# Attention's products with the values: from split parts in float32r to plain float32, two heads side by side in TensorE's column halves

## The chip, the cores and the metric

The kernel runs on one NeuronCore of a Trainium2 chip. The metric is the time of one execution on the device in microseconds (us), the median of several runs.

## The reference, cut to what matters

Three layers follow each other. The first is attention over 4 batches, 8 heads, 576 positions and 64 numbers per head, with rotary positions; it is the only layer that the change rewrites.

```python
q_rot, k_rot = (rotate(q), rotate(k))
scores = scale * np.matmul(q_rot, k_rot.transpose(0, 1, 3, 2))
scores = scores - np.max(scores, axis=-1, keepdims=True)
attn = np.exp(scores)
attn = attn / (np.sum(attn, axis=-1, keepdims=True) + 1e-09)
return np.matmul(attn, v).astype(np.float32)
```

Its output, with the heads put side by side, is the input of a gated feed-forward layer (`_moe_ref`), and that one's output is the input of a causal attention with four experts (`_moe2_ref`).

## The kernel before

The kernel has three stages, one for each layer. TensorE's fast format float32r rounds its operands, so each operand is split in a high part (rounded) and a low part (what rounding took away), and a product is made from two or three products of parts.

**Stage A, attention.** A *work* is a pair of heads of one batch: 16 works, numbered n = 0 to 15. A work has nine *slots* x = 0 to 8, one for each block of 128 query rows (blocks 0 to 3 of both heads in turn; slot 8 holds the last 64 rows of both). `slot(k)` writes the instructions of one slot, and they keep that order on each engine. In slot x of a work the kernel does these things, the stages of neighbouring blocks overlapping:

- `exps(x)`: ScalarE (ACT) reads the score bank `ps_S` and the negative row maximum `nmax` and writes the exponentials `e`.
- `turn(x-1)`: TensorE (PE) transposes the block before, four 128x128 pieces, `ps_t<-ident,e`.
- `scores(x+1)`: PE makes the next block's scores into one of the **two** `ps_S` banks (four products of 288 columns; six for x+1 = 8).
- `maxima(x+1)`: VectorE (DVE) takes the maximum of each row of that bank.
- `turn_left` (`ps_l`): five times a work PE transposes the last 64 columns of two blocks, which DVE has gathered (`gather`).
- `high`, `low`: ACT copies the transposed block, rounded, out of PSUM (`g00h`, `g01h` for the first 256 query rows of either head, `g1h` for the other 320 of both); DVE subtracts that from PSUM to get the low part (`g00l`, `g01l`, `g1l`). `left_high` and `left_low` do so for the left-over columns (`tlh`, `tll`).
- `av`: the products with the values, into `ps_o`, a single bank. `vst` holds the values' high part in its first 64 columns and the low part in the last 64, so one product of 128 columns gives both. A head's first 256 (or last 320) rows take ten products: five blocks of keys times two parts of the exponentials. They are written in two pieces, four products in one slot and six in the next: first half of the rows in slots 6, 7 and 8, 0; second half, for the work before, in slots 2, 3 and 4, 5.
- `av_out`: ACT copies `ps_o` to `xt`, and `store` writes it to memory (`xr`), high and low rows apart; they are added later.

`values` (ACT and GpSimd, POOL) makes `vst` from the loaded values `v`. Beside this, POOL rotates the queries and keys of the work after the next, DVE and POOL split them (`hi`, `lo`), DMAs on SyncE's queue (SP) spread the parts to the places where TensorE needs them, and in works with odd n the first layer's weights are unpacked (`wt`, four DVE operations and two of ACT for each of eight pieces, loaded into the single buffer `raw`).

**Stage B** starts with `attended`, which reads `xr` back, adds its two parts (`sa<-sa,sl`, on POOL), multiplies by the softmax factors (`sa<-sa,sr`) and splits the result (`xh`, `xl`). For batch 0 that already happens in stage A. **Stage C** is the third layer; no line of it is touched.

On each engine instructions run in the order in which they stand: a waiting one holds up all behind it.

Of the kernel before, what the change touches and what calls it, by code (L numbers as in the profile page):

```python
# [8 lines left out]
F32 = mybir.dt.float32  # L9
# [8 lines left out]
P = 128  # L18
HS = 288
NP = H // 2  # L20
NKB = 5
# [5 lines left out]
def f(ap):  # L27

    return ap.bitcast(F32)
# [11 lines left out]
def fused_kernel(ctx, tc, qk, v, w_in, w_out, w_sg, g_ln, b_sg, wqk, wvg, wo, rope, cst, out):  # L41
# [37 lines left out]
    xraw = [spill.tile([2, 4, P, S], F32, name=f"xr{b}") for b in range(B)]  # L79
# [200 lines left out]
    def attended(pool, b):  # L280


        ts = {}

        def load(c):
            ts[c] = a, l, r = [pool.tile([P, S], F32, tag="s" + x, name="s" + x, bufs=k)
                               for x, k in (("a", 3), ("l", 1), ("r", 1))]
            for x, t in enumerate((a, l)):
                nc.sync.dma_start(t, xraw[b][x, c])
            factor_in(r, rd[b][c])  # L290
            POOL.tensor_tensor(a, a, l, op=ALU.add)

        def norm(c):
            a, l, r = ts[c]
# [14 lines left out]

    def leftover(pool, b):  # L310

        a, l, r = [pool.tile([P, S], F32, tag="s" + x, name="e" + x, bufs=k)[:, 0:512]
                   .rearrange("p (c i n) -> p c i n", c=4, i=2) for x, k in (("a", 3), ("l", 1), ("r", 1))]
        for i in range(2):
            for x, t in enumerate((a, l)):
                nc.sync.dma_start(t[:, :, i, :], xraw[b + i][x, :, :, 512:S].rearrange("c p n -> p c n"))
# [4 lines left out]
        POOL.tensor_tensor(a, a, l, op=ALU.add)  # L321
# [13 lines left out]
    with ExitStack() as st:  # L335
# [12 lines left out]
        prs = [Pair(opd, x, zero, True) for x in range(2)]  # L348


        g0 = [[ptp.tile([P, 4, 256], F32R, name=f"g0{j}{x}") for x in "hl"] for j in range(2)]
        g1 = [ptp.tile([P, 4, 640], F32R, name="g1" + x) for x in "hl"]


        tl = [ptp.tile([P, 640], F32R, name="tl" + x) for x in "hl"]

        def ends(t):

# [6 lines left out]
        class Work:  # L365
# [17 lines left out]
                    nc.sync.dma_start(ident, cst[:, 0:P])  # L383

            def load_values(self):
                self.vt = ld.tile([P, NKB, 2, D], F32, tag="v", name="v", bufs=1)
                nc.sync.dma_start(self.vt, v[self.b, self.p])

            def first(self):
# [26 lines left out]
                else:  # L416
                    self.pr.fill_k(opd, hi, lo)

            def values(self):
                self.vst = ld2.tile([P, NKB, 2, P], F32R, tag="vst", name="vst")  # L420
                ACT.copy(self.vst[:, :, :, 0:D], self.vt)
                POOL.tensor_tensor(self.vst[:, :, :, D:P], self.vt, f(self.vst[:, :, :, 0:D]), op=ALU.subtract)

            def start(self):
                self.nmax, self.sums = [sm.tile([P, 9], F32, tag=x, name=x) for x in ("nmax", "sums")]
                self.ps, self.e, self.t4 = {}, {}, {}
# [24 lines left out]
                    PE.transpose(t4[:, kb, :], self.e[x][:, P * kb:P * kb + P], ident)  # L451

            def place(self, x):
                i, j = divmod(x, 2)
                hi, lo = g0[j] if i < 2 else g1
                off = P * i if i < 2 else P * (i - 2) + (320 if j else 64)
                if i < 4:
                    return self.t4[x], *[x[:, :, off:off + P] for x in (hi, lo)]
                return self.t4[x].rearrange("p k (j n) -> p k j n", j=2), *[ends(x) for x in (hi, lo)]
# [19 lines left out]
            def left_parts(self, second):  # L479
                c = slice(256, 640) if second else slice(0, 256)  # L480
                return self.l[:, 0:c.stop - c.start], *[x[:, c] for x in tl]

            def left_high(self, second):
                i, hi, lo = self.left_parts(second)
                ACT.copy(hi, i)

            def left_low(self, second):
                i, hi, lo = self.left_parts(second)
                DVE.tensor_tensor(lo, i, f(hi), op=ALU.subtract)

            def av(self, second, j, part):

                n = 320 if second else 256
                if part == 0:
                    self.o = bank("o")
                mms = [(self.vst[:, kb, j, :], g1[x][:, kb, 320 * j:320 * j + n] if second else g0[j][x][:, kb])
                       for x in range(2) for kb in range(4)]
                mms += [(self.vst[:, 4, j, :], t[:, 256 + 64 * j:S + 64 * j] if second else t[:, 0:256]) for t in tl]
                for x, (w, m) in enumerate(mms):
                    if (x >= 4) == part:  # L500
                        PE.matmul(self.o[:, 0:n], w, m, start=(x == 0), stop=(x == len(mms) - 1))

            def av_out(self, second, j):
                n = 320 if second else 256
                if j == 0:
                    self.xt = wk.tile([P, 2, n], F32, tag=f"xt{n}", name="xt", bufs=1)
                todo = [(0, 0, n)]
                if second and j == 0:
                    todo = [(256, 0, 64), (0, 64, 256)]
                for c, i, m in todo:  # L510
                    ACT.copy(self.xt[:, j, c:c + m], self.o[:, i:i + m])

            def factor(self, step):
                if step == 0:
# [8 lines left out]
            def store_factor(self):  # L523
                factor_out(wk, self.l[0:9, 384:512], rd[self.b][self.p])

            def store(self, second):
                c = slice(256, S) if second else slice(0, 256)
                for x in range(2):
                    nc.sync.dma_start(xraw[self.b][x, self.p].rearrange("(j p) s -> p j s", j=2)[:, :, c],
                                      self.xt[64 * x:64 * x + 64])  # L530

        def slot(k):


# [32 lines left out]
            if n == 0 and x == 3:  # L567
                works[1].rope(1, (2,), DVE)
            if wk:
                wk.high(xk)  # L570
                wk.low(xk)
            if x == 0 and p:
                p.factor(1)
            if x == 2 and p:
                p.left_high(True)
                p.store_factor()
                p.left_low(True)
            if x == 5 and w:
                w.left_high(False)
                w.left_low(False)  # L580
# [24 lines left out]

# [17 lines left out]
        works[1].load(1)  # L623
        fixed[0] = True
        works[1].rope(0)
        works[0].values()
        works[1].load_values()
        works[1].rope(1, (0, 1))
        works[0].start()
        works[0].scores(0)  # L630
# [806 lines left out]
```

## Time and profile before

| | |
|---|---|
| median of 3 runs | 738.38 us (736.77 to 738.62) |
| the profiled execution | 739.81 us, of which the profile's span is 738.0 us |
| busy shares over the span | PE 92%, weight loads (PEld) 86%, DVE 77%, ACT 64%, POOL 53% |
| DMA | 121.51 MB, 165 GB/s in the mean |
| stage A | about 0 to 300 us |

A profile is one execution as the hardware profiler saw it. Times in it count from the span's start. Matmuls are pipelined, and their recorded durations overlap; what a matmul costs TensorE is the distance to the next one's start. The chain of waits follows back from the last instruction to what released it, step by step. The clock is the one that the throttle granted to TensorE (1.00 is full).

### The profile page before, as it was taken

Reading aid. Unit: us, or ns where it says so; the run is one execution under the profiler, and the core shown is the slowest. Engines: PE = TensorE matmul, PEld = TensorE weight load, DVE = VectorE, ACT = ScalarE, POOL = GpSimd, SP = SyncE. Lnnn points to the kernel's source line nnn. Section 1 sums busy time; section 2 is a strip of 40 time slices with the busy share of each in tenths; the row PEclk is TensorE's granted clock in tenths of the full one; section 3 lists DMA queues with packets and bytes.
Section 4 is the critical chain, followed back from the end, with each engine's and each line's share of the span. In section 5 each row is a group of like instructions: output and inputs, shape, how many; then the busy total and the mean of one; then the engine's idle time right before and its main releaser. Section 6 shows DMA issues by size and latency. Waiting matters only on the chain.

```text
span 738.0 us, 14204 instructions
## 1 busy us (share of the span) xinstructions
PE 679.6 (92%) x4813; PEld 636.6 (86%) x4813; DVE 566.1 (77%) x1234; ACT 471.0 (64%) x1183; POOL 391.5 (53%) x311
## 2 busy tenths in 40 slices
PE   6899998987899999989779999998998989999987
PEld 6788898987798988888669999898998979999975
DVE  5799999996999999588996676556337786766774
ACT  7688898986798988543343442564226756666662
POOL 2798888986889962455624835603503340432220
PEclk9899999999999999999999999999999999999999
DMA  6689878879688963534546444304465354443521
GB/s 241 191 232 275 261 218 268 230 237 272 177 240 250 246 180 111 146 127 139 184 143 203 129 134 143 90 1 149 104 196 136 93 144 117 108 119 75 138 74 65
DMA packets 70410, 121.51 MB, mean 165 GB/s; under 512 B 19489, under 2 KB 28546, under 8 KB 70338
## 3 DMA queue, kind: packets, MB, share of 16 engines
q1 hardware_dynamic: 67602, 114.93, 53.6%
q10 hardware_dynamic: 2736, 5.68, 2.5%
q8 instruction: 39, 0.64, 0.4%
q14 instruction: 33, 0.27, 0.1%
HBM read 63.20 MB, written 23.70 MB: 118 GB/s over the span
## 4 chain that ended last, share of the span: by engine, by line
PE 55%; DVE 26%; ACT 6%; DMA 5%; POOL 3%; issue 3%; SPq 1%; DVEq 0%; ACTq 0%; POOLq 0%
PE ps_S L55 31%; PE ps_t L55 9%; PE ps_o L55 9%; DVE nmax L55 5%; DVE wt L55 4%; PE ps_f L55 4%; POOL t L55 2%; PE ps_s L55 2%; DVE g1l L55 2%; DVE hi L55 2%; ACT e L55 2%; ACT qz L55 2%; DVE g01l L55 1%; DVE g00l L55 1%; DVE e L55 1%
## 5 line engine op out<-in xcount | busy, mean ns | idle before, releaser
L55 PE MATMUL ps_t<-ident,e 128*128 128x128 f32 x776 | 127.2, 281 | 21.9 <-ACT e L55 17.6
L55 ACT ACTIVATE e<-ps_S,nmax 128x576 f32<-128x576 f32 x144 | 108.2, 751 | 31.6 <-DVE nmax L55 30.5
L55 PEld LDWEIGHTS ps_t<-ident,e 128*128 128x128 f32 x776 | 92.1, 143 | 35.8 <-ACT e L55 26.5
L55 DVE TENSOR_REDUCE nmax<-ps_S 128x1 f32<-128x576 f32 x144 | 107.5, 746 | 13.6 <-PE ps_S L55 11.5
L55 POOL TENSOR_TENSOR t<-t,rp 128x576 f32<-128x576 f32 x61 | 91.5, 1521 | 14.3 <-ACT rp L55 9.2
L55 PE MATMUL ps_S<-kh,q 128*128 128x288 f32 x352 | 85.1, 335 | 2.5 <-ACT kh L55 2.4
L55 PE MATMUL ps_S<-lo,qz 128*128 128x288 f32 x304 | 66.6, 301 | 1.5 <-DVE lo L55 1.5
L55 POOL TENSOR_TENSOR lo<-t,hi 128x576 fp32r<-128x576 f32 x30 | 43.0, 1433 | 33.0 <-DVE hi L55 33.0
L55 DVE TENSOR_TENSOR g1l<-ps_t,g1h 128x512 fp32r<-128x512 f32 x80 | 54.6, 683 | 2.2 <-ACT g1h L55 2.0
L55 PEld LDWEIGHTS ps_S<-kh,q 128*128 128x128 f32 x352 | 53.4, 195 | 2.8 <-ACT kh L55 2.5
L55 ACT ACTIVATE e<-e,nmax 128x128 f32<-128x128 f32 (+4 forms) x72 | 42.3, 587 | 21.0 <-DVE nmax L55 20.7
L55 POOL TENSOR_TENSOR yl<-x,yh 128x640 fp32r<-128x640 f32 x16 | 25.0, 1568 | 55.5 <-ACT yh L55 35.8
L55 PEld LDWEIGHTS ps_S<-lo,qz 128*128 128x128 f32 x304 | 49.9, 193 | 1.7 <-DVE lo L55 1.7
L55 POOL TENSOR_TENSOR xl<-sa,xh 128x576 fp32r<-128x576 f32 x16 | 27.2, 1711 | 38.5 <-ACT xh L55 38.5
L55 ACT CAST g1h<-ps_t 128x512 fp32r<-128x512 f32 x80 | 47.2, 590 | 0.0
L55 ACT ACTIVATE ga<-ga 128x512 f32<-128x512 f32 (+1 forms) x34 | 22.3, 657 | 33.4 <-DVE ga L55 33.2
L55 POOL TENSOR_TENSOR t<-t 128x576 f32<-128x576 f32 x29 | 41.8, 1441 | 2.3
L55 DVE CUSTOM_DVE_ANT_0 e<-ps_s,mask 128x128 f32<-128x128 f32 (+3 forms) x64 | 31.0, 486 | 8.7 <-PE ps_s L55 8.3
L55 POOL TENSOR_TENSOR xt<-xt,r 128x256 f32<-128x256 f32 (+1 forms) x14 | 11.3, 805 | 48.9 <-DMA r<-d 48.9
L55 PE MATMUL ps_S<-wsh,vh 128*128 128x288 f32 x160 | 34.9, 300 | 2.3 <-DVE u L55 1.8
L55 PE MATMUL ps_S<-xh,wih 128*128 128x288 f32 x128 | 29.1, 311 | 7.0 <-DVE gv L55 4.4
L55 PE MATMUL ps_S<-wsl,vh 128*128 128x288 f32 x160 | 34.1, 294 | 0.0
(296 smaller groups left out, 2204.9 us busy)
## 6 DMA issues: line engine op xcount, KB each, us to landing
t<-in_qk_dram SPq DMA_DIRECT2D x32, 576.0 KB
kh<-hi SPq DMA_DIRECT2D x92, 144.0 KB
q<-hi SPq DMA_DIRECT2D x38, 144.0 KB
qz<-hi SPq DMA_DIRECT2D x38, 144.0 KB
q<-lo SPq DMA_DIRECT2D x38, 144.0 KB
v<-in_v_dram SPq DMA_DIRECT2D x16, 320.0 KB
xr<-xt SPq DMA_DIRECT2D x32, 160.0 KB
sa<-xr SPq DMA_DIRECT2D x16, 288.0 KB
```

The lines of the kernel that those rows point to most:

```text
L55: ins = op(*a, **k)
```

## The change

Exponentials and values are no longer split. A transposed block is copied once, as plain float32, by ACT or, for x = 1, 4 and 7, by DVE. The values are used as loaded, `v` with two buffers in place of one, and loaded in slot 5. The products with the values are plain float32 with 64 columns of weights: head 0 writes partitions 0 to 63 of `ps_o`, head 1 partitions 64 to 127, in turn, so that both heads of a pair stand side by side in the array's column halves. All ten products of one half of the rows stand in one slot: slot 3 for the second half of the work before, slot 6 for the first half. `av_out` and `store` follow at the start of slots 4 and 7. `xr` holds one part, and the addition on POOL is gone in `attended` and `leftover`.

```diff
         def load(c):
-            ts[c] = a, l, r = [pool.tile([P, S], F32, tag="s" + x, name="s" + x, bufs=k)
-                               for x, k in (("a", 3), ("l", 1), ("r", 1))]
-            for x, t in enumerate((a, l)):
-                nc.sync.dma_start(t, xraw[b][x, c])
+            ts[c] = a, r = [pool.tile([P, S], F32, tag="s" + x, name="s" + x, bufs=k) for x, k in (("a", 3), ("r", 1))]
+            nc.sync.dma_start(a, xraw[b][c])
             factor_in(r, rd[b][c])
-            POOL.tensor_tensor(a, a, l, op=ALU.add)
...
             def load_values(self):
-                self.vt = ld.tile([P, NKB, 2, D], F32, tag="v", name="v", bufs=1)
+                self.vt = ld.tile([P, NKB, 2, D], F32, tag="v", name="v")
...
-            def values(self):
-                self.vst = ld2.tile([P, NKB, 2, P], F32R, tag="vst", name="vst")
-                ACT.copy(self.vst[:, :, :, 0:D], self.vt)
-                POOL.tensor_tensor(self.vst[:, :, :, D:P], self.vt, f(self.vst[:, :, :, 0:D]), op=ALU.subtract)
...
             def place(self, x):
+
                 i, j = divmod(x, 2)
-                hi, lo = g0[j] if i < 2 else g1
+                o, t = g0[j] if i < 2 else g1, self.t4[x]
...
-            def high(self, x):
-                i, hi, lo = self.place(x)
-                ACT.copy(hi, i)
-
-            def low(self, x):
-                i, hi, lo = self.place(x)
-                DVE.tensor_tensor(lo, i, f(hi), op=ALU.subtract)
+                (DVE.tensor_copy if x % 3 == 1 else ACT.copy)(o, t)
...
-            def av(self, second, j, part):
+            def av(self, second):
 
                 n = 320 if second else 256
-                if part == 0:
-                    self.o = bank("o")
...
+                self.o = bank("o")
+                for kb in range(NKB):
+                    for j in range(2):
+                        if kb == 4:
+                            m = tl[:, 256 + 64 * j:S + 64 * j] if second else tl[:, 0:256]
+                        else:
+                            m = g1[:, kb, 320 * j:320 * j + n] if second else g0[j][:, kb]
+                        PE.matmul(self.o[64 * j:64 * j + 64, 0:n], self.vt[:, kb, j, :], m, start=(kb == 0), stop=(kb == 4))
...
-            for at, g, second, j in ((1, p, False, 1), (4, p, True, 0), (6, p, True, 1), (8, w, False, 0)):
+            for at, g, second in ((4, p, True), (7, w, False)):
                 if x == at and g:
-                    g.av_out(second, j)
-            if x in (1, 6) and p:
-                p.store(x == 6)
+                    g.av_out(second)
+                    g.store(second)
...
-            for at, g, second, j in ((2, p, True, 0), (4, p, True, 1), (6, w, False, 0), (8, w, False, 1), (-1, p, False, 1)):
-                if x in (at, at + 1) and g:
-                    g.av(second, j, x - at)
+            for at, g, second in ((3, p, True), (6, w, False)):
+                if x == at and g:
+                    g.av(second)
...
-                if x == 6:
-                    nx.values()
-                    if n + 2 < B * NP:
-                        works[n + 2].load_values()
+                if x == 5:
+                    nx.load_values()
```

What this does to the order is seen best on TensorE. These are its rows of the kernel before from slot 3 to slot 6 of a work (`ps_t` transposes, `ps_S` scores, `ps_l` left-overs, `ps_o` products with the values):

```order
L55 MATMUL ps_o<-g1h,vst 128x320 x4
L55 MATMUL ps_t<-ident,e 128x128 x4
L55 MATMUL ps_S<-kh,q_1_172 128x288 x2
L55 MATMUL ps_S<-lo_410,qz_173 128x288 x2
L55 MATMUL ps_l<-ident,e 128x128
L55 MATMUL ps_o<-g1l,vst 128x320 x4
L55 MATMUL ps_o<-tlh,vst 128x320
L55 MATMUL ps_o<-tll,vst 128x320
L55 MATMUL ps_t<-ident,e 128x128 x4
L55 MATMUL ps_S<-kh,q_1_172 128x288 x2
L55 MATMUL ps_S<-lo_410,qz_173 128x288 x2
L55 MATMUL ps_o<-g00h,vst 128x256 x4
```

Four or six products with the values stand between any two blocks. In the changed kernel the same place of a work, from slot 3 to slot 6 (`g_196` is `g1`, `g_194` is the first of `g0`), reads:

```order
L55 MATMUL ps_o<-g_196,v 64x320 x8
L55 MATMUL ps_o<-tl,v 64x320 x2
L55 MATMUL ps_t<-ident,e 128x128 x4
L55 MATMUL ps_S<-kh,q_1_172 128x288 x2
L55 MATMUL ps_S<-lo_808,qz_173 128x288 x2
L55 MATMUL ps_l<-ident,e 128x128
L55 MATMUL ps_t<-ident,e 128x128 x4
L55 MATMUL ps_S<-kh,q_1_172 128x288 x2
L55 MATMUL ps_S<-lo_808,qz_173 128x288 x2
L55 MATMUL ps_l<-ident,e 128x128
L55 MATMUL ps_t<-ident,e 128x128 x4
```

All ten products of both heads now stand in one piece, and between the next blocks nothing stands but one left-over.

On SP's queue the load of the values stood behind the loads of queries and keys and ahead of a load of weights (`raw`). Before, at the change from work 8 to 9:

```order
L529 DMA xr_64<-xt 64x2x320 x2
L374 DMA t_2714<-in_qk_dram 128x1152
L374 DMA t_2716<-in_qk_dram 128x1152
L387 DMA v<-in_v_dram 128x640
L227 DMA raw<-in_w_in_dram 128x1024
L529 DMA xr_65<-xt 64x2x256 x2
```

In the changed kernel, at the same place:

```order
L492 DMA xr_64<-xt 64x320
L382 DMA v<-in_v_dram 128x640
L369 DMA t_2354<-in_qk_dram 128x1152
L369 DMA t_2356<-in_qk_dram 128x1152
L492 DMA xr_65<-xt 128x256
L227 DMA raw<-in_w_in_dram 128x1024
```

The values moved ahead, and `raw` now stands behind the store of the first half's output.

## Rows read from the trace of the kernel before

**Rows 1.** Busy us by stretch: PE, PEld, DVE, ACT, POOL; clock, DMA share, GB/s.
```profile
100.00:120.00 20.00, 19.19 (x150) 18.22 (x149) 19.09 (x37) 18.05 (x47) 18.81 (x14) 1.00 0.87 246
...
440.00:460.00 20.00, 20.00 (x152) 20.00 (x151) 13.33 (x19) 6.79 (x11) 9.44 (x7) 1.00 0.37 125
```

**Rows 2.** Chain of waits in 87 to 121 us: start, length, what.
```profile
95.36 0.11 PE ps_l L55
95.47 0.59 PE ps_o L55 x4
96.05 0.44 PE ps_t L55 x4
96.49 0.53 PE ps_S L55 x4
...
97.13 0.88 PE ps_o L55 x6
...
99.92 0.80 PE ps_S L55 x6
...
102.51 0.48 PE ps_o L55 x4
...
104.06 0.71 PE ps_o L55 x6
```

**Rows 3.** ACT's timeline, the one `rs` of each work, in its slot 0.
```profile
87.88 0.20 ACT L55 ACTIVATE rs<-sums 128x9 f32<-128x9 f32 x1
...
104.07 0.20 ACT L55 ACTIVATE rs<-sums 128x9 f32<-128x9 f32 x1
...
121.21 0.20 ACT L55 ACTIVATE rs<-sums 128x9 f32<-128x9 f32 x1
...
171.81 0.20 ACT L55 ACTIVATE rs<-sums 128x9 f32<-128x9 f32 x1
...
196.43 0.20 ACT L55 ACTIVATE rs<-sums 128x9 f32<-128x9 f32 x1
```

**Rows 4.** The tile `rs`: durations (min/median/max ns), first and last start.
```profile
L55 ACT ACTIVATE rs<-sums x16: 198/201/228, 37.2 to 295.7; 128x9 f32<-128x9 f32 x16
```

**Rows 5.** TensorE's warm-up by forms, plain float32, 5.4 to 6.6 and 1 to 9 us.
```profile
L55 PE MATMUL ps_l<-zero 128*128 128x128 f32 x13 | 1.6, 275 | 0.0
...
L55 PE MATMUL ps_l<-zero 128*64 128x128 f32 x32 | 2.0, 276 | 0.0
L55 PEld LDWEIGHTS ps_l<-zero 128*64 128x64 f32 x32 | 1.7, 137 | 0.1
```

**Rows 6.** Groups of 0 to 330 us: busy us, mean ns of one.
```profile
L55 DVE TENSOR_TENSOR g1l<-ps_t,g1h 128x512 fp32r<-128x512 f32 x80 | 54.6, 683 | 2.2 <-ACT g1h L55 2.0
...
L55 DVE SCALAR_TENSOR_TENSOR wt<-raw,wt 128x512 int32<-128x512 int32 x16 | 20.1, 1254 | 0.0
```

**Rows 7.** The tile `ob`: a plain float32 copy by DVE.
```profile
L55 DVE COPY ob<-ps_f x1: 693/693/693, 723.0 to 723.0; 128x512 f32<-128x512 f32 x1
```

**Rows 8.** Timeline, 101 to 104 and 152 to 153.5 us: from scores to transposes.
```profile
101.73 0.51 PE L55 MATMUL ps_S<-kh,q 128*128 128x288 f32 x2
...
102.55 0.76 DVE L55 TENSOR_REDUCE nmax<-ps_S 128x1 f32<-128x576 f32 x1 [0.30 <-PE ps_S L55]
...
103.34 0.74 ACT L55 ACTIVATE e<-ps_S,nmax 128x576 f32<-128x576 f32 x1 [0.18 <-DVE nmax L55]
...
152.44 0.74 ACT L55 ACTIVATE e<-ps_S,nmax 128x576 f32<-128x576 f32 x1 [0.95 <-DVE nmax L55]
...
153.32 0.31 PEld L55 LDWEIGHTS ps_t<-ident,e 128*128 128x128 f32 x3 [1.01 <-ACT e L55]
```

**Rows 9.** Chain of waits in work 9, 165 to 185 us.
```profile
171.21 6.96 DMA raw<-in_w_in_dram
```

**Rows 10.** Timeline of stage B, POOL and PE.
```profile
348.11 1.89 POOL L55 TENSOR_TENSOR sa<-sa,sl 128x576 f32<-128x576 f32 x1
...
355.64 0.50 PE L55 MATMUL ps_t<-wih,xl 128*128 128x512 f32 x1 [2.27 <-POOL xl L55]
```

More of the change, by code (lines that the diff above doesn't have):

```diff
@@ L77, in fused_kernel @@
     ident = cpool.tile([P, P], F32, name="ident")
-    xraw = [spill.tile([2, 4, P, S], F32, name=f"xr{b}") for b in range(B)]
+    xraw = [spill.tile([4, P, S], F32, name=f"xr{b}") for b in range(B)]
     rd = [spill.tile([4, 9, P], F32, name=f"rd{b}") for b in range(B)]
@@ L310, in leftover @@
     def leftover(pool, b):
-        a, l, r = [pool.tile([P, S], F32, tag="s" + x, name="e" + x, bufs=k)[:, 0:512]
-                   .rearrange("p (c i n) -> p c i n", c=4, i=2) for x, k in (("a", 3), ("l", 1), ("r", 1))]
+        a, r = [pool.tile([P, S], F32, tag="s" + x, name="e" + x, bufs=k)[:, 0:512]
+                .rearrange("p (c i n) -> p c i n", c=4, i=2) for x, k in (("a", 3), ("r", 1))]
         for i in range(2):
-            for x, t in enumerate((a, l)):
-                nc.sync.dma_start(t[:, :, i, :], xraw[b + i][x, :, :, 512:S].rearrange("c p n -> p c n"))
+            nc.sync.dma_start(a[:, :, i, :], xraw[b + i][:, :, 512:S].rearrange("c p n -> p c n"))
             for j in range(2):
@@ L320, in leftover @@
                 nc.sync.dma_start(r[h, :, i, :], d.to_broadcast([64, 4, 64]))
-        POOL.tensor_tensor(a, a, l, op=ALU.add)
         yield
@@ L348, in fused_kernel @@
         prs = [Pair(opd, x, zero, True) for x in range(2)]
-        g0 = [[ptp.tile([P, 4, 256], F32R, name=f"g0{j}{x}") for x in "hl"] for j in range(2)]
-        g1 = [ptp.tile([P, 4, 640], F32R, name="g1" + x) for x in "hl"]
-        tl = [ptp.tile([P, 640], F32R, name="tl" + x) for x in "hl"]
+        g0 = [ptp.tile([P, 4, 256], F32, name=f"g0{j}") for j in range(2)]
+        g1 = ptp.tile([P, 4, 640], F32, name="g1")
+        tl = ptp.tile([P, 640], F32, name="tl")
         def ends(t):
@@ L454, in place @@
                 i, j = divmod(x, 2)
-                hi, lo = g0[j] if i < 2 else g1
+                o, t = g0[j] if i < 2 else g1, self.t4[x]
                 off = P * i if i < 2 else P * (i - 2) + (320 if j else 64)
                 if i < 4:
-                    return self.t4[x], *[x[:, :, off:off + P] for x in (hi, lo)]
-                return self.t4[x].rearrange("p k (j n) -> p k j n", j=2), *[ends(x) for x in (hi, lo)]
-            def high(self, x):
-                i, hi, lo = self.place(x)
-                ACT.copy(hi, i)
-            def low(self, x):
-                i, hi, lo = self.place(x)
-                DVE.tensor_tensor(lo, i, f(hi), op=ALU.subtract)
+                    o = o[:, :, off:off + P]
+                else:
+                    o, t = ends(o), t.rearrange("p k (j n) -> p k j n", j=2)
+                (DVE.tensor_copy if x % 3 == 1 else ACT.copy)(o, t)
             def gather(self, i):
@@ L477, in turn_left, with place_left @@
                 PE.transpose(o, self.e[2 * i][:, 512:640], ident)
-            def left_parts(self, second):
+            def place_left(self, second):
                 c = slice(256, 640) if second else slice(0, 256)
[L481 to L489, printed above, removed]
@@ L491, in av @@
-            def av(self, second, j, part):
-                n = 320 if second else 256
-                if part == 0:
-                    self.o = bank("o")
[L496 to L501, printed above, removed]
@@ L503, in av_out @@
-            def av_out(self, second, j):
-                n = 320 if second else 256
[L505 to L511, printed above, removed]
+                ACT.copy(tl[:, c], self.l[:, 0:c.stop - c.start])
@@ new lines, in av @@
+            def av(self, second):
+                n = 320 if second else 256
+                self.o = bank("o")
[3 more added lines that the diff above has]
+                            m = tl[:, 256 + 64 * j:S + 64 * j] if second else tl[:, 0:256]
+                        else:
+                            m = g1[:, kb, 320 * j:320 * j + n] if second else g0[j][:, kb]
+                        PE.matmul(self.o[64 * j:64 * j + 64, 0:n], self.vt[:, kb, j, :], m, start=(kb == 0), stop=(kb == 4))
@@ new lines, in av_out, with store @@
+            def av_out(self, second):
+                n = 320 if second else 256
+                self.xt = wk.tile([P, n], F32, tag=f"xt{n}", name="xt", bufs=1)
+                ACT.copy(self.xt, self.o[:, 0:n])
+            def store(self, second):
+                o, t = xraw[self.b][self.p], self.xt
+                if second:
+                    todo = [(o[0:64, 256:512], t[0:64, 64:320]), (o[0:64, 512:S], t[0:64, 0:64]), (o[64:P, 256:S], t[64:P, :])]
+                else:
+                    todo = [(o[:, 0:256], t)]
+                for a, c in todo:
+                    nc.sync.dma_start(a, c)
@@ L524, in store_factor @@
                 factor_out(wk, self.l[0:9, 384:512], rd[self.b][self.p])
[L526 to L530, printed above, removed]
         def slot(k):
@@ L569, in slot @@
             if wk:
-                wk.high(xk)
-                wk.low(xk)
+                wk.place(xk)
             if x == 0 and p:
@@ L574, in slot @@
             if x == 2 and p:
[L575 removed]
+                p.place_left(True)
                 p.store_factor()
[L577 removed]
             if x == 5 and w:
[L579 to L584 removed]
+                w.place_left(False)
+            for at, g, second in ((3, p, True), (6, w, False)):
+                if x == at and g:
+                    g.av(second)
             if nx:
@@ L625, in fused_kernel @@
         works[1].rope(0)
-        works[0].values()
-        works[1].load_values()
         works[1].rope(1, (0, 1))
```

2 lines of the change are left out of this document (1 added, 1 removed).

## The prediction

> **What bounds the kernel now.** I read the busy time by stretch first. In stage A all engines are full [rows 1]: of 20 us TensorE is busy 19.2, VectorE 19.1, ScalarE 18.1 and POOL 18.8; in stage B TensorE is busy throughout and the others wait for it. So the change must pay in stage A, and busy shares don't say on which engine. The chain of waits does. In works with even n, where no weights are unpacked, it runs on TensorE alone, block after block [rows 2]: 0.44 us of transposes, 0.53 of scores (0.80 where six products make them), 0.11 for a left-over, and a piece of the products with the values, 0.59 and 0.88 us for the second half of the rows, 0.48 and 0.71 for the first. One work has 9 x 0.44 + 8 x 0.53 + 0.80 + 6 x 0.11 (five left-overs and the factors) = 9.66 us without the values, and 2 x (0.59 + 0.88 + 0.48 + 0.71) = 5.32 with them: 14.98 us of TensorE. A work takes 16.2 us where n is even (87.88 to 104.07) and 17.1 where it is odd [rows 3]; the extra is VectorE's, which unpacks weights in between. Over works 1 to 15 it is 258.5 us [rows 4], one of them, work 9, with 24.6 [rows 3]. So TensorE is 1.2 us (n even) and 2.1 us (n odd) of a work from its own floor, and relief of the other engines can bring no more than that, unless TensorE's work itself shrinks.
>
> **TensorE's work after the change.** Twenty products in plain float32 with 64 columns of weights take the place of forty in float32r. The trace has this form, in the warm-up. A plain float32 matmul is issued as two pieces. With the full array 13 of 128 columns take 1.6 us [rows 5], (1.6 - 0.275) / 12 = 0.11 us a piece. In column halves 32 pieces take 2.0 us: as the last one's 0.276 is mostly its own length, 16 steps in some 1.75 us, 0.11 us for two pieces. So the halves do run side by side, and two heads cost what one would. With the columns in proportion (the fixed part of a step counted along, so this is the upper end; without any, 4% less) a pair of pieces takes 0.22 us at 256 columns and 0.275 at 320. Ten pairs each: 2.2 and 2.75 us. Going into the halves and out of them, four times a work, has no row of its own: between nothing and one weight load that lies open, 0.137 us [rows 5]; I take 0.09, nearer the upper end, since the array has to run empty: 0.36. Sum 9.66 + 4.95 + 0.36 = 14.97 us. TensorE's work stays what it was.
>
> By the Trainium skill's page TensorE: Matmul & The Clock Gate (Part 3, on packing small matmuls) a weight load overlaps running matmuls only where their row groups differ, which halves of the columns do not offer; by it every step would also pay a weight load, and the sum would be the 790 us of the third rival. Here 32 loads of 0.137 us, 4.4 us in all, lie within the 2.0 us of their matmuls [rows 5], so the trace speaks against it.
>
> **What the others are relieved of.** VectorE loses nine subtractions of 0.68 us [rows 6] and two smaller ones, and gains three copies; the nearest row for such a copy, out of PSUM at the end of the kernel, says 0.69 [rows 7]. That is 4 to 5 us of a work. ScalarE loses a third of its copies, the rounding of the values and half of `av_out`, and POOL the values' low part. None of this counts by itself: as the sum above shows, TensorE would still need 14.97 us. It matters by what TensorE waits for.
>
> **What is late next.** The two score banks allow a lead of one block. From the start of a block's scores 0.82 us pass to the maxima (101.73 to 102.55), 0.79 to the exponentials, 0.88 to the block's first transposes (152.44 to 153.32) [rows 8]: 2.49 us, in which TensorE must find other work. In order it has that block's own scores (0.53), the transposes of the block before (0.44) and the scores of the block after (0.53), 1.50 us, and what else stands in these two slots. So for each two neighbouring blocks TensorE waits 0.99 us, less what else stands there. Before the change there is a piece of the products with the values in eight slots of nine, 0.48 to 0.88 us, and so almost every such sum is covered. After it, slots 3 and 6 have everything, and the others a left-over of 0.11, or (slot 1) two. The sums of neighbouring waits, by the slot in which the later block's scores stand: slots 4 and 5, 0.99 - 0.22 = 0.77; 7 and 8, 0.88 (the six products of slot 7 lengthen both sides); 8 and 0, 0.88; 0 and 1, 0.66; 1 and 2, 0.77; none across slots 3 and 6. The least that satisfies all is 0.77 + 0.88 + 0.77 = 2.42 us. Followed in order, with ScalarE's `xt` copy standing ahead of the exponentials of slots 4 and 7 so that they wait for the burst, I get 2.5. A work then takes 14.97 + 2.5 = 17.5 us, against 16.2.
>
> In the eight odd works an operation of the unpacking stands on VectorE between the maxima of slot 8's block and the next. Before, it lengthened VectorE's row; now VectorE is idle in the bursts, and only this place counts: of its 1.25 us [rows 6] 0.83 would reach TensorE, 0.27 if it runs undisturbed by POOL; I take 0.55. That makes 18.05 against 17.1.
>
> **What comes back.** Work 9 lost 7.5 us: ScalarE waited for weights whose load was issued behind the values' load, which waited for POOL, and took 6.96 us to land [rows 9]. Now the values wait for nobody, but the load stands behind the store of slot 7, which waits for the burst. It is issued about 0.9 us after the second burst (the copy `xt`, the store) and lands 7 us later; ScalarE comes to it in slot 1, by the working above some 6 us after the burst. I leave 1.9 us of the loss. In stage B POOL's addition of 1.89 us stands ahead of the `xl` for which TensorE waited 2.27 us [rows 10]; without it TensorE starts 1.9 earlier, and as it is full later on [rows 1], that stays. The other additions lie beside a busy TensorE and give nothing. The store's third DMA and the values' load now stand ahead of the loads of queries and keys; I cost them at nothing, since their rotation is used only in slots 1 and 3 of the next work, some 8 us later; were that cover gone, it is the second rival below.
>
> **The sum.** Works 1 to 15: 7 x 17.5 + 8 x 18.05 + 1.9 = 268.8, against 258.5: +10.3. Less 1.9 in stage B: +8.4. The profiled execution, 739.8 (span 738.0 and 1.8 around it), becomes 748.2; the median of the runs lies 1.4 lower, so 746.8. I say 746.5.
>
> **The rivals.**
> *TensorE is kept fed* (the other side). What must fall is the 2.5 us a work. For it: these waits are sums of latencies, and a shorter queue on VectorE and ScalarE shortens them; TensorE may also load weights of the next scores during a wait. Against it: the three latencies are already those of places where no queue stood before. If half of them goes, 15 x 1.25 = 19 us come off: 728. If all goes, 709. It decides from waits under 2.5 - 8.4 / 15 = 1.9 us a work.
> *The queue slips.* Loads of queries and keys come behind three stores that wait for the burst; if the rotation on POOL is late for slots 1 and 3, 1 us a work more: 762.
> *The halves don't overlap so well with real operands.* In the warm-up both halves read one tile; here each has its own. With weight loads in the open, 20 steps x 0.137 = 2.7 us a work, 790. With the halves one after the other, 4.95 us a work, 826. Against it stand the warm-up's rows.
>
> **How the numbers follow.** A measurement of this kernel tells about 0.3% from no change, 2.2 us. Forecast (waits as worked out, 738 to 757): 0.54, of which 0.46 slower, 0.06 the same and 0.02 faster. TensorE fed, 709 to 738: 0.26, of which 0.03 the same. The queue: 0.12. Halves: 0.08. So slower 0.66, same 0.09, faster 0.25. The forecast's own range, 738 to 757, follows from 0.3 us a work either way for the latencies and 0.27 to 0.83 for the unpacking. For 8 in 10 the range reaches to half of the waits, with a little beyond for a faster work 9, and to the queue's case: 726 to 763; outside lie the halves' 0.08 and the ends of the two others.
>
> **What would show it.** Right: steps of 0.22 and 0.275 us in the products with the values; busy VectorE and ScalarE in stage A well below 15 of 20 us; transposes waiting for exponentials some 2.5 us a work, mainly in slots 5, 6, 8, 1 and 2 and none after slots 3 and 6; works of 17 to 18 us; work 9 no longer apart. Wrong: works under 16.5 us with TensorE without gaps, or bursts of 5 us and more.

## The result and the profile after

| | before | after |
|---|---|---|
| median | 738.36 us (736.77 to 738.62, 4 runs) | 746.65 us (745.91 to 751.36, 4 runs) |
| ratio after to before | | 1.013, 95% interval 1.0086 to 1.0175 |
| span of the profiled execution | 738.0 us | 744.5 us |
| first and last of the 16 `rs` | 37.2 and 295.7 us | 35.3 and 312.4 us |
| from the last `rs` to the end | 442.3 us | 432.1 us |

The kernel became slower by 1.3%, 8.3 us, where 746.5 us were predicted. The two last lines show that this is a difference of two larger numbers: works 1 to 15 take 18.6 us more (277.1 against 258.5), and what follows takes 10.2 less; 1.9 more came back ahead of work 0's `rs`, where the granted clock of the kernel before was 0.50 from 28.9 to 32.3 us and the changed kernel's 1.00 (no run separates the two). The prediction had +10.3 and -1.9 in the two main places, so its sum stands on two errors of opposite sign.

Busy time by stretch (PE, PEld, VectorE, ScalarE, POOL), answering [rows 1]:

```profile
100.00:120.00 20.00, 17.72 (x131) 13.20 (x130) 12.55 (x25) 13.22 (x35) 12.81 (x10) 1.00 0.68 188
440.00:460.00 20.00, 20.00 (x152) 20.00 (x151) 15.29 (x35) 8.68 (x15) 4.67 (x3) 1.00 0.35 110
```

In stage A no engine is full any more. VectorE falls from 19.1 to 12.6 of 20 us, ScalarE from 18.1 to 13.2, and TensorE, which nothing relieved, from 19.2 to 17.7: it waits. The period of a work, from ScalarE's timeline and the tile's summary (durations in ns, first and last start), answering [rows 3, 4]:

```profile
71.84 0.20 ACT L55 ACTIVATE rs<-sums 128x9 f32<-128x9 f32 x1
90.71 0.20 ACT L55 ACTIVATE rs<-sums 128x9 f32<-128x9 f32 x1
108.20 0.20 ACT L55 ACTIVATE rs<-sums 128x9 f32<-128x9 f32 x1
127.06 0.20 ACT L55 ACTIVATE rs<-sums 128x9 f32<-128x9 f32 x1
145.48 0.20 ACT L55 ACTIVATE rs<-sums 128x9 f32<-128x9 f32 x1
```
```profile
L55 ACT ACTIVATE rs<-sums x16: 198/201/218, 35.3 to 312.4; 128x9 f32<-128x9 f32 x16
```

A work with odd n takes 18.87 us (71.84 to 90.71), one with even n 17.49 (90.71 to 108.20). Works 6, 8 and 10 take 18.4 to 18.7 (127.06 to 145.48). The chain of waits through half a work, answering [rows 2]:

```profile
75.66 0.66 PE ps_t L55 x4
76.31 0.53 PE ps_S L55 x4
76.84 2.84 PE ps_o L55 x20
79.69 0.59 PE ps_t L55 x4
80.27 0.55 PE ps_S L55 x4
...
80.85 0.77 DVE nmax L55
...
81.70 0.84 ACT e L55 x2
...
82.58 0.66 PE ps_t L55 x4
83.24 0.53 PE ps_S L55 x4
83.77 2.31 PE ps_o L55 x20
```

Before, the chain ran on TensorE alone. Now it leaves TensorE once between the two bursts: scores at 80.27, maxima, exponentials, and the block's transposes at 82.58. The bursts themselves take 2.84 and 2.31 us, and the transposes behind them 0.59 where they took 0.44 [rows 2]. What TensorE waits for from 30 to 300 us, by the table of waits (us in total, times, longest):

```profile
PE ps_t L55 <- ACT e L55: 28.5, 59, 1.4
```

### The profile page after: what moved, and what is told of

Same layout as the page of the kernel before. It is cut to its first block, busy times and chain, and to the rows that moved or that the text cites. A ratio compares the mean times of both kernels' runs of the same rounds, so it can differ in the third digit from the quotient of the medians.

```text
span 744.5 us, 13802 instructions
## 1 busy us (share of the span) xinstructions
PE 681.0 (91%) x4813; PEld 587.1 (79%) x4813; DVE 486.6 (65%) x1106; ACT 428.3 (58%) x1071; POOL 336.6 (45%) x277
## 4 chain that ended last, share of the span: by engine, by line
PE 65%; DVE 17%; ACT 10%; issue 3%; DMA 3%; POOL 1%; SPq 1%; ACTq 0%; DVEq 0%; POOLq 0%
PE ps_S L55 32%; PE ps_o L55 15%; PE ps_t L55 12%; ACT e L55 5%; DVE nmax L55 5%; PE ps_f L55 4%; DVE wt L55 3%; PE ps_s L55 2%; DMA raw<-in_w_in_dram 2%; ACT qz L55 2%; DVE e L55 1%; ACT wt L55 1%; DVE ga L55 1%; DMA qz<-hi 1%; DVE sa L55 1%
## 5 line engine op out<-in xcount | busy, mean ns | idle before, releaser
L55 PE MATMUL ps_t<-ident,e 128*128 128x128 f32 x776 | 129.6, 284 | 38.9 <-ACT e L55 36.8
L55 PEld LDWEIGHTS ps_t<-ident,e 128*128 128x128 f32 x776 | 86.8, 141 | 79.0 <-ACT e L55 61.2
L55 POOL TENSOR_TENSOR t<-t,rp 128x576 f32<-128x576 f32 x61 | 88.0, 1464 | 14.2 <-ACT rp L55 9.2
L55 PE MATMUL ps_o<-g,v 128*64 128x320 f32 (+1 forms) x512 | 69.2, 412 | 0.0
L55 ACT COPY g<-ps_t 128x512 f32<-128x512 f32 x96 | 55.5, 579 | 0.2 <-PE ps_t L55 0.2
L55 PEld LDWEIGHTS ps_o<-g,v 128*64 128x64 f32 x512 | 34.0, 137 | 24.4 <-issue 5.3
L55 ACT COPY xt<-ps_o 128x256 f32<-128x256 f32 (+1 forms) x32 | 12.8, 399 | 63.3 <-PE ps_o L55 63.3
```

The lines of the kernel that those rows point to most:

```text
L55: ins = op(*a, **k)
```

## The experiments

Each is the changed kernel with an edit, except the one marked as the kernel before. Those of one run only (2, 7, 9 and 10) are read by their traces. Ratios are to the kernel before, run beside them. "Works" are distances between `rs`; "even" is a work with even n and nothing of batch 0's multiplication in it.

**1. The bursts dealt out over eight slots.**

```diff
+        PARTS = ((0,), (1,), (2,), (3, 4))
-                for kb in range(NKB):
+                for kb in PARTS[part]:
-            for at, g, second in ((4, p, True), (7, w, False)):
+            for at, g, second in ((5, p, True), (0, p, False)):
-            for at, g, second in ((3, p, True), (6, w, False)):
-                if x == at and g:
-                    g.av(second)
+            for at, g, second in ((1, p, True), (5, w, False)):
+                if 0 <= x - at < 4 and g:
+                    g.av(second, x - at)
```

> The changed kernel, with each burst of products dealt out over four slots: keys' blocks 0, 1, 2 and 3 with 4 in slots 1 to 4 (second half of the rows) and 5 to 8 (first half). Theory (TensorE waits because most slots have no filler): the waits for exponentials, 2.7 us in a work with even n, nearly all go; TensorE's own work rises by the six further times that it goes into the column halves and out of them, 0.05 + 0.09 us each, to 9.66 + 4.91 + 1.12 = 15.7 us. Works of 15.7 to 16.1 us (even) and at most 17 (odd), in place of 17.5 and 18.9; 746.7 less 7 x 1.6 less 8 x 1.9 = 720 us, between 712 and 728. First rival (the waits come from queues on VectorE and ScalarE, not from missing filler): works stay at 17.3 or more, 743 to 750. Second rival (going into and out of the halves costs far more once it happens eight times a work): works of 18 us and more, over 750.

Measured: 729.76 us, ratio 0.987 (0.9839 to 0.9902). A stretch of the chain of waits:

```profile
90.10 0.59 PE ps_t L55 x4
90.68 0.53 PE ps_S L55 x4
91.21 0.69 PE ps_o L55 x4
91.90 0.58 PE ps_t L55 x4
...
103.30 0.64 PE ps_t L55 x4
```

The chain is on TensorE alone again, and works with odd and with even n take the same 17.08 us: the waits are gone but for 0.2 us (below), and with them the price of the unpacking. So the first rival (queues on VectorE and ScalarE) falls. The expected 15.7 us a work was too low, because each trip into the column halves costs more than the 0.14 us that I had read at the two ends of a burst. A slot now takes 0.59 + 0.53 + 0.69 = 1.81 us, with 0.15 of the trip in the transposes behind it. Two kernels give both unknowns. In the changed one products and two trips cost 2.84 + 2.31 + 2 x 0.15 = 5.45 us. In this one 17.08 - 9.66 = 7.42 us hold the products, eight trips and 0.20 us of slot 0, where no piece stands and the transposes take 0.64 in place of 0.44 (the last row). A trip is (7.42 - 0.20 - 5.45) / 6 = 0.30 us, the products alone 4.9. Works 6, 8 and 10 took 17.96: VectorE's multiplication for batch 0 stands between two blocks' maxima at the end of slot 8, where slot 0 has no products.

**2. One head after the other.**

```diff
-                for kb in range(NKB):
-                    for j in range(2):
+                for j in range(2):
+                    for kb in range(NKB):
```

> The changed kernel, with all five products of head 0 ahead of the five of head 1 in a burst; nothing else. Theory (the two column halves run at the same time, and only neighbouring pieces of different halves overlap): the pieces of one head follow each other at 0.269 and 0.222 us, so the bursts take up to 20 x 0.269 = 5.4 and 20 x 0.222 = 4.4 us in place of 2.84 and 2.31; at 4.7 us more in each of 15.5 works about 815 us, 790 to 825. Rival (a piece of 64 columns takes half the time of a full one wherever it stands): bursts as before, 746 us.

Measured: 792.56 us. TensorE's timeline of one burst:

```profile
83.37 2.42 PE L55 MATMUL ps_o<-g,v 128*64 128x320 f32 x10
85.57 0.43 PE L55 MATMUL ps_o<-tl,v 128*64 128x320 f32 x1
85.63 0.43 PE L55 MATMUL ps_o<-g,v 128*64 128x320 f32 x1
85.84 0.43 PE L55 MATMUL ps_o<-tl,v 128*64 128x320 f32 x1
85.90 1.51 PE L55 MATMUL ps_o<-g,v 128*64 128x320 f32 x5
87.25 0.70 PE L55 MATMUL ps_o<-tl,v 128*64 128x320 f32 x2
87.88 0.66 PE L55 MATMUL ps_t<-ident,e 128*128 128x128 f32 x4
```

Head 0 has eight pieces `g` and two `tl`. Its eight take 85.57 - 83.37 = 2.20 us, 0.275 each, and five of head 1 take 87.25 - 85.90 = 1.35, 0.27 each: one piece alone costs what a pair costs when the heads take turns (below). So the halves do work at the same time, and only pieces of different halves that stand close to each other overlap; the rival falls. The time is below the expected 815 because TensorE doesn't keep strictly to the order in which the products are written: ten `g` have begun by 85.57, two of them of head 1, and the two `tl` of head 0 stand between further `g` of head 1. Some four steps overlap at the seam. The burst is 4.51 us long in place of 2.85, the other one 3.66 in place of 2.31 (91.95 to 95.61); together 3.0 more, and works with even n go from 17.48 to 20.49.

**3. The unpacking and batch 0's multiplication behind the bursts.**

```diff
-            if x in ((1, 3, 4, 6, 7, 8) if n % 2 else (7,)):
-                next(wload, None)
+            for at in ((3, 3, 3, 6, 6) if n % 2 else (3, 3) if n else (7,)):
+                if x == at:
+                    next(wload, None)
-            if n >= 4 and x == 8:
+            if n >= 5 and x == 6:
```

> The changed kernel, with the unpacking of the weights and the steps of batch 0's multiplication moved to the end of slots 3 and 6, behind the bursts, where VectorE and ScalarE stand idle for 1.5 to 2.9 us. Theory (these operations cost time only because they stand between two blocks' maxima or ahead of exponentials, 1.4 us in odd works and 0.9 at the starts of works 6, 8 and 10): all works go to 17.4 to 17.8 us, 8 x 1.3 + 3 x 0.9 = 13 us less, 734 us (731 to 738). Rival (they cost time through the engine's load or its shared port, wherever they stand): no change, 743 to 750.

Measured: 741.88 us, ratio 1.0044 (1.0016 to 1.0071): 4.8 us less than the changed kernel, not 13. Works 6, 8 and 10 fell to 17.7, as the other even ones, though the multiplication takes 1.36 us here: beside a burst it costs nothing (experiment 7 shows what it meets at its old place). Odd works fell to 18.33 only, and the other even ones, which now hold two steps of the unpacking in place of one, rose from 17.48 to 17.69. VectorE's timeline in slot 3:

```profile
77.22 3.17 DVE L55 TENSOR_SCALAR wt<-wt 128x512 f32<-128x512 f32 x2 [0.22 <-ACT wt L55]
80.31 1.43 DVE L55 TENSOR_REDUCE nmax<-ps_S 128x1 f32<-128x576 f32 x2
```

Two operations, 0.42 and 1.25 us long in the changed kernel, take 3.17 here, while POOL is busy throughout, and outlast the burst; the maxima of the next block come behind them.

**4. POOL's additions put back.**

```diff
             factor_in(r, rd[b][c])
+            POOL.tensor_tensor(pool.tile([P, S], F32, tag="sl", name="sl", bufs=1), a, a, op=ALU.subtract)
```

(and the same in `leftover`).

> The changed kernel with an operation on POOL put back where the additions stood (a subtraction of the same shape from itself into the tile that held the low part, its result unused, no further load). It prices the additions alone. Theory (the additions held up VectorE and POOL at the start of stage B beyond the one place that was costed): stage A unchanged (277 us from work 0 to work 15), the way from there to the first steady products of stage B longer by 6 to 9 us, 753 to 756 us. Rival (only the one addition ahead of the late low part counts; the rest of what stage B regained comes from elsewhere, such as weights unpacked further ahead): 748 to 750 us.

Measured: 753.74 us, ratio 1.0197 (1.0157 to 1.0237): 7.1 us more than the changed kernel. Stage A is nearly as it was: 278.0 us from the first to the last `rs`, against 277.1, with 0.9 more in work 9. Behind the last `rs` the profiled execution takes 755.5 - 313.1 = 442.4 us, as long as before the change. But it was the slowest of the four (757.26 us), and not all of that is stage B's (see below).

**5. The products in five pieces.** As in experiment 1, with these pieces (slots and blocks of keys), `av_out` at the start of slots 4 and 0, and the multiplication of batch 0 at the end of slot 5:

```diff
+            for at, g, second, kbs in ((1, p, True, (0, 1)), (3, p, True, (2, 3, 4)), (5, w, False, (0, 1)), (7, w, False, (2, 3)), (8, w, False, (4,))):
+                if x == at and g:
+                    g.av(second, kbs)
```

> The changed kernel, with the products in five pieces: second half of the rows in slots 1 (keys' blocks 0, 1) and 3 (2, 3, 4), first half in slots 5 (0, 1), 7 (2, 3) and 8 (4), so that of any two neighbouring slots one has a piece; the steps of batch 0's multiplication at the end of slot 5. From the traces so far a trip into the column halves and out of them costs TensorE 0.31 us whatever the piece holds: (17.08 - 9.66 - 4.91) / 8. Theory (a wait goes once one of the two slots that it spans has a piece of products): TensorE's own work 9.66 + 4.91 + 5 x 0.31 = 16.1 us and no waits; 15 works of 16.1 to 16.4 us in place of 17.1 to 18.0 with eight pieces, 729.8 - 14 = 716 us, 712 to 721. Rival (a wait needs filler in both slots, since each block is late by its own): works of 16.8 and more, over 724.

Measured: 718.01 us (716.7 to 721.99), ratio 0.9727 (0.9686 to 0.9768). Even works take 16.45 us, odd ones 16.6, or 17.0 where the multiplication runs.

```profile
L55 ACT ACTIVATE rs<-sums x16: 206/209/214, 34.5 to 282.3; 128x9 f32<-128x9 f32 x16
```

One piece in either of two neighbouring slots is enough. By 9.66 + 4.9 + 5 x 0.30 = 16.1, some 0.4 us of waits are left. This kernel is faster than both others, by 2.7% and 3.8%.

**6. In four pieces,** in slots 2, 4, 6 and 8, with `av_out` at the start of slots 5 and 0 and the multiplication of batch 0 at the end of slot 6.

> The changed kernel, with the products in four pieces: second half in slots 2 (keys' blocks 0, 1) and 4 (2, 3, 4), first half in slots 6 (0, 1) and 8 (2, 3, 4); the steps of batch 0's multiplication at the end of slot 6. Theory: own work 9.66 + 4.91 + 4 x 0.31 = 15.8 us, and the one pair of neighbouring slots without a piece, 0 and 1, waits 0.66 us: 16.5 us a work, some 719 us, 714 to 726. Rival as for five pieces: 17 and more, over 728.

Measured: 724.79 us, ratio 0.9811 (0.9774 to 0.9849). Most works take 16.2 to 16.6 us, as expected; the three odd ones in which the multiplication runs take 18.45, 1.9 us more, since it now stands with an operation of the unpacking between the maxima of two blocks, and is itself 1.97 us long (at 114.05 us).

**7. One operation of the unpacking from slot 7 to slot 6.**

```diff
-            if x in ((1, 3, 4, 6, 7, 8) if n % 2 else (7,)):
+            for at in ((1, 3, 4, 6, 6, 8) if n % 2 else (7,)):
```

> The changed kernel, with one operation of the unpacking (VectorE's second combination of words, 0.98 us) moved from the end of slot 7 to the end of slot 6, beside the burst. Theory (in odd works 0.83 us of the 1.4 come from this operation between the maxima of two blocks, the other 0.57 from ScalarE's operation that stands ahead of the exponentials in slot 2): works with odd n go from 18.87 to about 18.05, even ones stay, 8 x 0.83 = 6.6 us less, 740 us. First rival (the extra is ScalarE's alone): no change, 746. Second rival (the extra is VectorE's alone): 17.5, 735.

Measured: 745.96 us; odd works 18.67, 0.2 less in place of 0.8. VectorE's timeline:

```profile
84.67 3.04 DVE L55 SCALAR_TENSOR_TENSOR wt<-raw,wt 128x512 int32<-128x512 int32 x2
87.63 0.74 DVE L55 TENSOR_REDUCE nmax<-ps_S 128x1 f32<-128x576 f32 x1
```

The two operations take 3.04 us side by side, and so the maxima behind them are late by nearly as much as before. The burst's cover is 2.3 us. The works around moved too, which nobody expected: works 6 and 8, with the multiplication for batch 0 at its old place, fell from 18.41 to 17.49 (explained below), while work 9 rose from 19.69 to 21.07.

**8. The kernel before, without POOL's additions** (both lines `a, a, l, op=ALU.add` left out).

> The kernel before, without POOL's additions of the low part of attention's output (that part of the result is left out; its loads stay). It prices the additions where they stood. Theory (they hold up VectorE and POOL at the start of stage B by 8 to 9 us, and in the changed kernel this hides half of what stage A loses): stage A nearly as before, 738.4 - 8 = 730 us, 727 to 733. Rival (1.9 us, as one addition ahead of one late low part): 736 to 737.

Measured: 733.8 us (730.64 to 736.25), ratio 0.9939 (0.9911 to 0.9966): 5.0 us less (2.5 to 6.6), between the two theories. In its profiled execution the part behind the last `rs` takes 729.8 - 294.9 = 434.9 us, 7.4 less than before.

**9. ScalarE's operation of the unpacking from slot 1 to slot 3** (`(3, 3, 4, 6, 7, 8)` for odd n).

> The changed kernel, with ScalarE's first operation of the unpacking (the absolute value, 0.57 us) moved from the end of slot 1 to the end of slot 3, beside the burst. Theory (it delays the exponentials of slot 2 by its own length, and that part of the 1.4 us goes wherever it has cover): works with odd n go from 18.87 to 18.3, 8 x 0.55 = 4.4 us less, 742 us. Rival (VectorE's operations, stretched beside POOL, decide odd works alone): 18.87 as before, 746.

Measured: 745.02 us; odd works 18.53, so this operation, moved, gives back 0.34 of the 1.39 us and not 0.55. Work 9 takes 18.53 too: where the operation that waits for `raw` stands later, nothing of its loss is left.

**10. A fifth of the products.**

```diff
-                for kb in range(NKB):
+                for kb in range(1):
```

(and `start` and `stop` true for that one product).

> The changed kernel, with one block of keys out of five in each burst (four fifths of the products with the values are left out). Theory (TensorE's waits are the latency from scores to exponentials that no other work fills, and the burst is not their cause): the waits of 2.3 us stay, a little more behind the shorter bursts; works with even n 17.48 - 0.8 x 4.91 = 13.55 to 13.9 us, some 688 us. Rival (the waits come from the bursts, behind which VectorE and ScalarE must catch up): they shrink with the burst, works of 9.66 + 0.98 + 0.62 + 0.5 = 11.8 us, some 659 us.

Measured: 716.15 us, more than both expectations, since a new wait came in. TensorE's timeline and its windows (PE, PEld, VectorE, ScalarE, POOL, granted clock):

```profile
71.58 0.66 PE L55 MATMUL ps_t<-ident,e 128*128 128x128 f32 x4 [0.59 <-ACT e L55]
...
76.34 0.66 PE L55 MATMUL ps_t<-ident,e 128*128 128x128 f32 x4 [0.33 <-ACT e L55]
...
99.60 0.82 PE L55 MATMUL ps_S<-kh,q 128*128 128x288 f32 x2 [4.55 <-DMA kh<-hi]
```
```profile
99.60:102.60 3.00, 3.00 (x13) 2.88 (x13) 1.35 (x2) 0.87 (x4) 0.04 (x1) 0.50 0.58 137
103.20:106.20 3.00, 2.18 (x17) 1.66 (x15) 2.37 (x7) 2.65 (x7) 0.85 (x1) 1.00 0.89 319
```

Where works would take under 15 us, the next work's keys are late (4.55 us), while POOL is busy throughout (4.52 us from 95.00 to 99.60). It is close to the prediction's second rival, which the changed kernel's works of 17.5 us don't meet: its table of waits from 30 to 300 us has TensorE wait for a DMA once, for 0.2 us. Four odd works without that wait serve the comparison: 14.62 to 14.80 us, against 18.87 - 0.8 x 4.9 = 14.9 if the waits stay, and 1.4 + 11.8 = 13.2 if they shrink with the burst. The waits themselves say the same: ahead of the transposes of slots 3 and 6 TensorE waits 0.59 and 0.33 us in work 3 (the first two rows), and in the same places of the changed kernel 0.58 and 0.34. Nor is it ScalarE's copy `xt`, which stands ahead of exponentials and waits for the burst: 56.7 us in all in the changed kernel from 30 to 300 us, 2.5 here from 30 to 270. So the bursts fill waits; they don't make them.

## Why the prediction came out right, point by point

**TensorE's work.** The steps were right: eight pairs of pieces go from 76.77 to 78.98, 0.276 us a pair, and from 83.70 to 85.48, 0.2225; 0.275 and 0.22 were predicted.

```profile
76.77 2.37 PE L55 MATMUL ps_o<-g,v 128*64 128x320 f32 x16
78.98 0.71 PE L55 MATMUL ps_o<-tl,v 128*64 128x320 f32 x4
...
83.70 1.95 PE L55 MATMUL ps_o<-g,v 128*64 128x256 f32 x16
85.48 0.60 PE L55 MATMUL ps_o<-tl,v 128*64 128x256 f32 x4
...
94.89 2.37 PE L55 MATMUL ps_o<-g,v 128*64 128x320 f32 x16
...
113.13 2.37 PE L55 MATMUL ps_o<-g,v 128*64 128x320 f32 x16
```

The trips were taken at 0.36 us a work and measured 0.60, 0.15 at either end of a burst, above the upper bound of 0.137; the products alone at 4.95 and measured 4.9. TensorE's own work is 9.66 + 5.45 = 15.1 us, against 14.97. The rival with the halves one after the other is out by the steps, and so is the one with weight loads in the open: the page's group of these loads has a mean of 137 ns, so 20 of them, 2.7 us in all, lie within a burst of 2.84 whose steps are those of the columns.

```profile
L55 PEld LDWEIGHTS ps_o<-g,v 128*64 128x64 f32 x512 | 34.0, 137 | 24.4 <-issue 5.3
```

**The waits.** 17.48 - 15.1 = 2.4 us in an even work, against 2.5. Experiments 1, 5 and 10 show the cause: filler in one of two neighbouring slots takes the wait away, in neither it stays, and the burst is not its source. Of the places, "none after slots 3 and 6" was right; of slots 5, 6, 8, 1 and 2, only slot 6. In work 4 TensorE waits 0.71, 0.41, 0.03 and 0.34 us ahead of the transposes of slots 0, 3, 5 and 6, and behind such a wait four transposes take 0.66 in the place of 0.44: 2.4 us in all. Slot 2 waits in odd works only (0.30) and slot 1 in even ones only (0.33), both behind the unpacking. So the sum of the waits was right, and the slots to which it was dealt were mostly not. 17.5 us for an even work was right to 0.02, with 0.1 more of work and 0.1 less of waits.

**VectorE and ScalarE** were relieved as predicted, and in the changed kernel it brought nothing: TensorE waits longer. With the waits filled, in experiment 5, odd works take 16.6 us where they took 17.1 before the change.

**Odd works** is the first term that was mis-sized: "+0.55" measured 1.39. The step counted one place, the operation between the maxima of slot 8's block and the next. ScalarE's operation ahead of the exponentials of slot 2 adds 0.34 (experiment 9), and moving operations beside the bursts takes away 0.20 (experiment 7) or, all together, 0.33 of an odd and an even work (experiment 3: 18.33 + 17.69 against 18.87 + 17.48). The rest could not be assigned operation by operation: they were moved in groups, and grouped operations got longer. Over eight works this is some 7 us, in part made up by work 9.

The 1.39 us are not all the odd work's own. `rs` marks ScalarE, and it comes late behind an odd work. From burst to burst on TensorE a work takes 18.12 us (76.77 to 94.89 in the rows above) and the next 18.24 (94.89 to 113.13): the unpacking of an odd work holds up slot 2 of its own and slot 1 of the following one. Firm is the pair: 36.35 us, against 17.5 + 18.05 = 35.55.

**Work 9** kept 0.8 us of its loss, against 1.9 predicted: 19.69 us, against 18.87 in other odd works; ScalarE's wait for `raw` is 0.7 us. It is not firm: in experiment 4, which leaves this part of the kernel alone, work 9 takes 20.60.

**Works 6, 8 and 10** were not in the prediction: 0.9 us each and more, 3 us in all. VectorE's multiplication for batch 0 stood there before the change too, took 0.74 us, and works 6 and 8 took 16.7 in place of 16.2. In the changed kernel it begins beside an operation of POOL and takes 1.44, with the next maxima behind it (at 128.18). In experiment 7, at the same place, it begins ahead of POOL's operation, takes 0.75, and works 6 and 8 are no longer than other even ones (17.49); in work 10 it takes 1.84, and that work 18.87. So the place alone doesn't cost the 0.9 us; it comes with what POOL does there. The changed kernel, then experiment 7:

```profile
126.36 1.28 POOL L55 TENSOR_TENSOR wil<-wt,wih 128x512 fp32r<-128x512 f32 x1 [1.28 <-ACT wih L55]
126.82 1.44 DVE L55 TENSOR_TENSOR sa<-sa,sr 128x576 f32<-128x576 f32 x1
```
```profile
125.91 0.75 DVE L55 TENSOR_TENSOR sa<-sa,sr 128x576 f32<-128x576 f32 x1
126.04 1.76 POOL L55 TENSOR_TENSOR wil<-wt,wih 128x512 fp32r<-128x512 f32 x1 [0.90 <-DVE g L55]
```

**Stage B** is the second mis-sized term: "-1.9" measured -10.2, of which 0.6 stand in stage C. Stage B's share shows between the last `rs` and stage C's first `yl`. The tile `yl` before the change, after it, in experiment 4 and in experiment 8 (first and last start at the end):

```profile
L55 POOL TENSOR_TENSOR yl<-x,yh x16: 1544/1566/1599, 507.2 to 650.5; 128x640 fp32r<-128x640 f32 x16
L55 POOL TENSOR_TENSOR yl<-x,yh x16: 1543/1566/2086, 514.3 to 658.0; 128x640 fp32r<-128x640 f32 x16
L55 POOL TENSOR_TENSOR yl<-x,yh x16: 1545/1566/2087, 521.5 to 667.9; 128x640 fp32r<-128x640 f32 x16
L55 POOL TENSOR_TENSOR yl<-x,yh x16: 1552/1565/1628, 498.9 to 642.4; 128x640 fp32r<-128x640 f32 x16
```

That is 211.5 us before and 201.9 after, 9.6 less; with the additions put back 208.4, and before the change without them 204.0. So POOL's additions cost 6.5 to 7.5 us there (7.1 and 5.0 by the medians) and are the main cause; the other 2 to 3 us of the 9.6 are open. What experiment 4 loses beyond that, 3.8 us, stands in stage C, which has no such addition: there its granted clock was 0.50 from 514.8 to 518.0 and from 579.6 to 582.8 us, where the changed kernel's was 1.00.

The step looked only at what POOL itself did next (`xl`); TensorE's wait there is 1.90 us where it was 2.27 [rows 10]. It left out who else waits for POOL. One pair of rows of the kernel before, ahead of it, and the same operation of VectorE after:

```profile
320.81 1.44 POOL L55 TENSOR_TENSOR sa<-sa,sl 128x576 f32<-128x576 f32 x1
...
320.92 1.35 DVE L55 TENSOR_SCALAR y<-ii 128x5 int32<-128x5 int32 x1
```
```profile
336.96 0.17 DVE L55 TENSOR_SCALAR y<-ii 128x5 int32<-128x5 int32 x1
```

An operation of VectorE on 5 numbers a partition takes 1.35 us and ends with POOL's addition; without the addition it takes 0.17, and so it does in experiment 8 (at 320.11 us). The operation ahead of it, `ii<-w`, still takes 1.36 us beside POOL's multiplication. At the start of stage B the chain runs through VectorE, and from 316 to 364 us POOL had five such additions. The Trainium skill, SBUF — State Buffer, section "SBUF: two separate sides", says that VectorE, in some of its instructions, and GpSimd share one pair of ports, which the first to start holds for its whole instruction; these rows agree, and so do those of work 6 above.

**The sum.** +18.6 in the works (predicted +10.3), -10.2 behind them (-1.9), -1.9 ahead of them (0): +6.5 us in the profile, against +8.4. The mechanism in stage A was right, its price too small; the closeness of 746.65 to 746.5 is luck, since two errors of 8 us cancelled.

## What to carry to other kernels

When work is gathered into bursts, ask what filled the waits between the bursts: here the same products cost 746.7 us in two bursts, 729.8 in eight pieces and 718.0 in five (where batch 0's multiplication moved too), because each piece fills the wait of two neighbouring slots and each trip into another shape of the array costs 0.3 us. Relief of engines that are not last brings nothing until the waits that it was to shorten are counted. And an operation removed on POOL must be priced by what it held up on VectorE, not by its own queue alone: a VectorE operation between two maxima cost 0.9 us a work or nothing, by whether POOL's began before it.

## What was not expected of the hardware

- A trip of TensorE into column halves and back costs 0.30 us beyond the products, about half of it in the full-width transposes that follow (0.59 against 0.44). The Trainium skill, TensorEngine Tiling (Array Packing), section "Key Properties", says that changing the tiling mode drains the engine; the trace agrees in so far as a price shows at either end of a burst.
- Two column halves side by side bring the full factor of two: 0.27 us for one piece of 320 columns alone (experiment 2), 0.276 for two side by side. Where one head follows the other, TensorE begins pieces of the second ahead of the first one's last ones, for some four steps.
- After 4.55 us without work (experiment 10) the granted clock was 0.50, the lower level of 1.2 GHz, from 99.6 to 102.6 us, and full again from 103.2.
